# Weight rows in pairs, add and ReLU in one instruction, and another order in the first attention step

## The chip, the cores and the metric

The kernel runs on one core of a Trainium2 chip. Its metric is the device time of one execution in microseconds (us). The engines' names are those of the profile: PE does matrix multiplications (PEld is its loading of weights, instruction LDWEIGHTS), DVE is the vector engine, ACT the scalar engine, POOL the GpSimd engine, SP the sync engine. Matrix products land in PSUM, everything else lies in SBUF. POOL and SP issue DMAs here; POOL's convert fp32 in memory to fp16 in SBUF on the way.

## What is computed

A causal attention over 4 batches, 8 heads, 768 positions and 64 numbers per head, whose output feeds four experts that are all applied and mixed:

```python
is_retrieval = [1, 0, 1, 0, 0, 0, 1, 0]; n_sink, window = 4, 64
scores = q @ k.T / 8                  # per batch and head, 768 x 768
keep = causal                         # retrieval heads 0, 2, 6
keep = causal & (pos < 4 | rel < 64)  # the other, streaming heads
a = softmax(where(keep, scores, -1e9)); x = a @ v
x = x.transpose(0, 2, 1, 3).reshape(3072, 512)
p = domain_probs / (domain_probs.sum(-1) + 1e-9)
out = sum over e of p[:, e] * (relu(x @ w1[e]) @ w2[e])   # w1: 512 x 1024, w2: 1024 x 512
```

The output is fp32; products are taken in fp16 with fp32 accumulation.

## The kernel before

**Attention** is done in eight steps g = 2b + c, one for each batch b and each half c of its 768 positions (384 queries). `scores(h)` multiplies a head's keys and queries tile by tile into PSUM (L659), and ACT takes the exponential into an fp16 tile `es` (L677). For retrieval heads and c = 1 there are four such tiles, in the order of `score_tiles`: the first two cross the diagonal and are multiplied by a 0/1 mask on DVE (L681), the last two need no mask. In the first step (g = 0) the mask is added by a matmul instead (L671). `values(h)` multiplies the exponentials by v: for retrieval heads (`values_r`, L713) the result has a column with the sum, and DVE adds 1e-9, inverts and scales it (L738, L741, L742); for streaming heads (L785) the sums lie in PSUM beside the result, and ACT takes the logarithm (L803) and exp(-log) (L813; L818 for heads 3 and 4 of the first step together), after which DVE scales into `xT` (L808). That scaling is put off: `later` appends it to the list `behind`, and `tick` emits it on DVE when a planned 1.3 us have passed. `xT[g]` holds the step's output with the 512 columns in four tiles of 128 rows: tile 0 has heads 0 and 4, tile 1 heads 1 and 5, tile 2 heads 2 and 6, tile 3 heads 3 and 7. Retrieval heads' results have to be transposed to get there: in the first step by three matmuls with an identity and a copy on DVE (`x_transposes`, L762, L766). `both` interleaves two generators, step by step. PSUM tiles of the first step's values alternate between two buffers of `pV` and two of `pO`. The order of the first step's last part is written out by hand:

```python
yield from both(scores(6), values(4))
yield from both(scores(7), values(6))
yield from values(5)
yield from values(7)
x_transposes(6)
```

**The experts** work on 24 tiles of 128 rows of x. The first step's three tiles, and then the fourth alone, go through `plain_steps`, expert after expert: layer 1 (L1027: weights w1sb loaded, xT streamed with 384 or 128 columns) with the ReLU on ACT (L1040), layer 2 (L1048) with w2sb streamed, and the mix on DVE (L1060, L1064). The first four matmul groups of expert 0 take the column tiles in the order 0, 2, 1 for all four groups, and only then tile 3.

The other twenty tiles go in ten pairs through `pair_steps`. Layer 1 is a plain product (`plain_layer1`, L1154, 256 columns, ReLU on ACT L1163) for experts 0, 1, 2 in seven pairs and for experts 0, 1 in the last three; the rest, expert 3 or experts 2 and 3, are done with the seven products of Winograd's form (`winograd_layer1`, L1183), whose partial sums ACT keeps (L1193) and DVE adds (`add`: L1199) and cuts at zero (L1205). Layer 2 is the seven products over all experts at once (L1290). Between the pairs the attention steps 1 to 7 are fed in, piece by piece, by a plan.

**Loads of the weights** are all on POOL's queue, in an order written by hand, with `landed` (L502), a tiny copy on POOL that waits for an earlier load: w1 of expert 0, w2 of expert 0, w1 of 1, then `landed(w1_of(0))`, halves of the second step's k and q, `landed(w2_of(0))`, w2 of 1, and so on. `load_w1` makes two DMAs per expert with 2 KB rows in SBUF; `load_w2` (L339 to L343) one DMA with rows of 1 KB: SBUF partition p gets rows p, 128 + p, 256 + p, ... of w2[e], and the columns of w1 that are loaded for one LDWEIGHTS are accordingly 128 neighbours.

Of the kernel before, what the change touches and what calls it, by code (L numbers as in the profile page):

```python
# [9 lines left out]

# [8 lines left out]
def kernel(  # L19
# [311 lines left out]
    def load_w1(e, f0, f1):  # L331
        x = moe_w1[e].rearrange("(u c d) f -> u d c f", u=2, c=DMP)
        for u in range(2):
# [2 lines left out]
                in_=x[u, :, :, f0:f1],  # L336
            )

    def load_w2(e):  # L339
        gp.dma_start(  # L340
            out=w2sb[:, e * FTP : (e + 1) * FTP, :],
            in_=moe_w2[e].rearrange("(fo fi) d -> fi fo d", fi=P),
        )  # L343


    ONES = 0.0078125 * (1.0 + 15360.0 * 2.0**-23)
# [192 lines left out]
    def attention(b, c):  # L539
# [152 lines left out]
        def values_r(h):  # L692

            ct, u = PLACE[h]
            shared = by_dma and ct
            if not (shared and u):
                pv_of[0] = pV.tile([P, 512], FP32, name="pV", bufs=2)
            ps = pv_of[0]
            if first:
                warm_up(ps, {6: 6}.get(h, 0), 256)  # L700
            heads = ps.rearrange("p (u x) -> p u x", u=2)[:, :, 0 : 3 * (D + 2)]
            heads = heads.rearrange("p u (j x) -> p u j x", j=3)
            ps = heads[:, u if shared else 0, :, :]
            work = []
            for es, parts in es_of[h]:
                for t, o, q0, nq in parts:
                    for j in range(3):
                        x = j * P - q0
                        if 0 <= x < nq:
                            work.append((j, t, es[:, o + x : o + x + P]))  # L710
            ns = 0
            for n, (j, t, lhsT) in enumerate(work):
                nc.tensor.matmul(  # L713
                    out=ps[:, j, 0 : D + 1],
                    lhsT=lhsT,
                    rhs=vR[i][:, t, RH.index(h), 0 : D + 1],
                    start=(n == 0),
                    stop=(n == len(work) - 1),
                    skip_group_check=True,
                )  # L720
                ns += mm_ns(D + 1)
                if ns > 200 and n < len(work) - 1:
                    yield ns
                    ns = 0
            x = x_pair if ct else x_one
            if shared and not u:
                yield ns
                return
            if shared:
                rs = att.tile([P, 2, 3, 1], FP32, name="rs", bufs=2)  # L730
                sums, top = heads[:, :, :, D : D + 1], heads[:, :, :, 0:D]
                to = x.rearrange("p j (u d) -> p u j d", u=2)
                shape = [P, 2, 3, D]
            else:
                rs = att.tile([P, 2, 3, 1], FP32, name="rs", bufs=2)[:, 0, :, :]
                sums, top, to = ps[:, :, D : D + 1], ps[:, :, 0:D], x[:, :, half(u)]
                shape = [P, 3, D]
            nc.vector.tensor_scalar(  # L738
                out=rs, in0=sums, scalar1=1e-9, scalar2=None, op0=ALU.add
            )  # L740
            nc.vector.reciprocal(out=rs, in_=rs)  # L741
            nc.vector.tensor_tensor(  # L742
                out=to, in0=top, in1=rs.to_broadcast(shape), op=ALU.mult
            )
            yield ns
            if h != 2 and not first:
                nc.sync.dma_start(
                    out=xT[g][:, ct, :].rearrange("p (j x) -> p j x", j=3),
                    in_=x.rearrange("p j x -> p (j x)"),
                    transpose=True,  # L750
                )
# [85 lines left out]
        if first:  # L837
# [14 lines left out]
            yield from transposes(3)  # L852
            yield from values(1)
            yield from both(scores(5), values(3))
            yield from both(scores(6), values(4))
            yield from both(scores(7), values(6))
            yield from values(5)
            yield from values(7)
            x_transposes(6)
            tick(LAG)  # L860
            small_things()
        else:
# [83 lines left out]
    def tick(ns):  # L946
        clock[0] += ns
        while behind and behind[0][0] <= clock[0]:
            behind.pop(0)[1]()
# [64 lines left out]
    def plain_steps(nt0, tiles, e, tokens, n0):  # L1014
# [6 lines left out]
        for f0 in [0, *range(ahead, FTP)]:  # L1021
            pss = {ft: bank() for ft in range(f0, f0 + (1 if f0 else ahead))}
            cts = (0, 2, 1, 3)

            def layer1(ft, n):
                ct = cts[n]
                nc.tensor.matmul(  # L1027
                    out=pss[ft][:, 0:cols_n],
                    lhsT=w1sb[:, e * DMP + ct, ft * P : (ft + 1) * P],
                    rhs=x[:, ct, :],  # L1030
                    start=(n == 0),
                    stop=(n == DMP - 1),
                )

            for ft in pss:
                for n in range(DMP - 1):
                    layer1(ft, n)
            for ft, ps in pss.items():
                layer1(ft, DMP - 1)
                nc.scalar.activation(  # L1040
                    out=hs[:, ft, :], in_=ps[:, 0:cols_n], func=AF.Relu
                )
                yield DMP * mm_ns(cols_n), 0.6
# [88 lines left out]
    def first_sum(e, n=1):  # L1132
# [2 lines left out]
            out=S1[:, k, :], in0=A21[:, k, :], in1=A22[:, k, :], op=ALU.add  # L1135
        )


    PSHARE = 1.57

# [5 lines left out]
    def pair_steps(nt0, nxt):  # L1146

        def plain_layer1(e):
            xs = scaled(e)
            for f0 in range(0, FTP, 2):  # L1150
                ps = bank()
                for f in range(2):
                    for ct in range(DMP):
                        nc.tensor.matmul(  # L1154
                            out=ps[:, f * PC : (f + 1) * PC],
                            lhsT=w1sb[:, e * DMP + ct, (f0 + f) * P : (f0 + f + 1) * P],
                            rhs=xs[:, ct, :],
                            start=(ct == 0),
                            stop=(ct == DMP - 1),
                        )  # L1160
                b0 = 2 * (f0 // HT)
                k0 = e * HT + f0 % HT
                nc.scalar.activation(  # L1163
                    out=blocks[:, b0 : b0 + 2, k0 : k0 + 2, :].rearrange(
                        "p t f x -> p f t x"
                    ),
                    in_=ps.rearrange("p (f t x) -> p f t x", f=2, t=2),
                    func=AF.Relu,
                )
                yield 2 * DMP * mm_ns(PC), 0.5  # L1170
# [5 lines left out]
        def winograd_layer1(e, x, y):  # L1176
# [18 lines left out]
            def block(n):  # L1195
                return blocks[:, n, e * HT : (e + 1) * HT, :]

            def add(n, ps, b):
                nc.vector.tensor_tensor(  # L1199
                    out=block(b),  # L1200
                    in0=ps.rearrange("p (f x) -> p f x", f=HT),
                    in1=kept[n].rearrange("p (f x) -> p f x", f=HT),
                    op=ALU.add,
                )
                nc.vector.tensor_scalar(  # L1205
                    out=block(b), in0=block(b), scalar1=0.0, scalar2=None, op0=ALU.max
                )

            def t(n):
# [337 lines left out]
```

The softmax here doesn't subtract the row's maximum and nothing guards it: scores larger than these inputs give would overflow.

## Time and profile before

| | |
|---|---|
| three runs | 378.41, 378.68, 377.46 us, median 378.41 |
| profiled execution | 377.47 us; its span on the core 375.8 us |
| matmuls | 4128 |
| granted clock of PE | full over the whole span |
| w2 loads (L340) | 4, 11.7 to 16.5 us from issue to landing, median 12.5 |
| w1 loads (L334) | 8, 5.7 to 12.8 us, median 9.3 |
| mean DMA rate, 20 to 40 us | 201 GB/s |
| mean DMA rate, 60 us to the end | 89 GB/s |

The span is the time between the first and the last instruction on the core. Of PE it has to be known that matmuls are pipelined: a matmul's recorded time is that from its start to its end, while the next one has already started, so that "busy" hides short gaps. A timeline row merges neighbours of one kind ("x8"), and a bracket at its end says how long the engine had been idle before and what ended that.

### The profile page before, as it was taken

Reading aid. Unit: us, or ns where it says so; the run is one execution under the profiler, and the core shown is the slowest. Engines: PE = TensorE matmul, PEld = TensorE weight load, DVE = VectorE, ACT = ScalarE, POOL = GpSimd, SP = SyncE. Lnnn points to the kernel's source line nnn. Section 1 sums busy time; section 2 is a strip of 40 time slices with the busy share of each in tenths; the row PEclk is TensorE's granted clock in tenths of the full one; section 3 lists DMA queues with packets and bytes.
Section 4 is the critical chain, followed back from the end, with each engine's and each line's share of the span. In section 5 each row is a group of like instructions: output and inputs, shape, how many; then the busy total and the mean of one; then the engine's idle time right before and its main releaser. Section 6 shows DMA issues by size and latency. Waiting matters only on the chain.

```text
span 375.8 us, 10137 instructions
## 1 busy us (share of the span) xinstructions
PE 367.5 (98%) x4128; PEld 310.2 (83%) x4128; DVE 282.7 (75%) x620; ACT 227.8 (61%) x475; POOL 113.7 (30%) x155
## 2 busy tenths in 40 slices
PE   8889999999999999999999999999999999999996
PEld 4745466668998988999989898998899998999996
DVE  7774768697888679878758858967778868769572
ACT  3863478547785785765676955784777361450630
POOL 8934573882058038115601650320000000000000
PEclk9999999999999999999999999999999999999999
DMA  9999999999699599977904991951220300300101
GB/s 164 155 201 206 196 187 191 181 207 105 97 109 144 106 96 120 152 116 58 207 10 59 170 157 21 127 127 14 69 72 2 107 9 0 114 2 6 54 2 56
DMA packets 124771, 39.24 MB, mean 104 GB/s; under 512 B 113728, under 2 KB 118404, under 8 KB 124724
## 3 DMA queue, kind: packets, MB, share of 16 engines
q0 software_dynamic: 86848, 19.01, 59.1%
q1 hardware_dynamic: 36276, 19.18, 21.9%
q8 instruction: 32, 0.52, 0.6%
q10 hardware_dynamic: 1600, 0.39, 0.5%
q14 instruction: 15, 0.12, 0.1%
HBM read 44.89 MB, written 6.34 MB: 136 GB/s over the span
## 4 chain that ended last, share of the span: by engine, by line
PE 87%; DMA 7%; POOL 3%; DVE 2%; issue 0%; POOLq 0%
PE pO L1290 31%; PE pA L1154 25%; PE pO L1183 9%; DMA w2sb<-in_moe_w_dram 7%; PE pO L1048 6%; PE pA L659 5%; PE pA L1027 5%; PE pV L713 2%; PE pV L785 2%; PE pA L1183 2%; POOL vS L309 1%; POOL vR L303 1%; DVE xs L1112 1%; PE pA L1380 0%; POOL early L453 0%
## 5 line engine op out<-in xcount | busy, mean ns | idle before, releaser
L1290 PEld LDWEIGHTS <-hA 128*128 128x128 f16 x1104 | 104.9, 98 | 12.2
L1154 PE MATMUL pA<-xs,w1sb 128*128 128x256 f16 x864 | 109.3, 272 | 0.0
L1154 PEld LDWEIGHTS <-w1sb 128*128 128x128 f16 x864 | 80.7, 98 | 8.5
L1163 ACT ACTIVATE hA<-pA 128x512 f16<-128x512 f32 x108 | 64.4, 598 | 35.1 <-PE pA L1154 32.9
L1290 PE MATMUL pO<-w2sb,hA 128*128 128x256 f16 x640 | 76.7, 272 | 0.0
L677 ACT ACTIVATE es<-pA 128x384 f16<-128x384 f32 (+2 forms) x122 | 59.2, 511 | 27.1 <-PE pA L659 23.3
L305 POOL DMA_DIRECT2D vS<-in_v_dram x30 | 29.6, 989 | 111.7 <-PE pV L785 110.5
L1290 PE MATMUL pO<-tsb,hA 128*128 128x256 f16 x464 | 56.7, 272 | 0.0
L1112 DVE TENSOR_TENSOR xs<-xT,pB 128x1024 f16<-128x1024 f16 (+1 forms) x52 | 49.4, 969 | 1.2 <-DMA out_dram<-o 1.2
L967 DVE TENSOR_TENSOR hA<-hA 128x1024 f16<-128x1024 f16 x60 | 39.6, 684 | 0.4
L1040 ACT ACTIVATE hA<-pA 128x384 f16<-128x384 f32 (+1 forms) x64 | 22.2, 385 | 19.8 <-PE pA L1027 19.6
L1027 PE MATMUL pA<-xT,w1sb 128*128 128x384 f16 (+1 forms) x256 | 30.9, 273 | 1.3 <-DVE xT L766 0.8
L1048 PE MATMUL pO<-w2sb,hA 128*128 128x512 f16 x128 | 30.7, 379 | 0.3 <-DMA w2sb<-in_moe_w_dram 0.3
L1310 ACT COPY s<-pO 128x256 f32<-128x256 f32 x31 | 11.5, 372 | 27.7 <-PE pO L1290 21.9
L1027 PEld LDWEIGHTS <-w1sb 128*128 128x128 f16 x256 | 19.3, 98 | 10.2 <-issue 1.9
L808 DVE TENSOR_TENSOR xT<-pV,rc 64x384 f16<-64x384 f32 x37 | 20.5, 555 | 9.1 <-ACT rc L813 6.6
L1183 PEld LDWEIGHTS <-w1sb 128*128 128x128 f16 x416 | 26.3, 98 | 1.1 <-issue 0.2
L803 ACT ACTIVATE rc<-pV,eps 64x384 f32<-64x384 f32 x37 | 21.3, 576 | 6.5 <-PE pV L785 5.9
L1199 DVE TENSOR_TENSOR hA<-pO,s 128x512 f16<-128x512 f32 x26 | 17.9, 687 | 9.3 <-PE pO L1183 6.7
L681 DVE TENSOR_TENSOR es<-es,mS 128x384 f16<-128x384 f16 (+1 forms) x40 | 13.7, 343 | 13.4 <-ACT es L677 13.4
L659 PE MATMUL pA<-qT,kR 128*128 128x384 f16 (+2 forms) x120 | 22.9, 278 | 0.6 <-DVE kR L576 0.6
L1193 ACT COPY s<-pO 128x512 f32<-128x512 f32 x39 | 22.5, 585 | 1.4 <-PE pO L1183 1.2
(144 smaller groups left out, 498.2 us busy)
## 6 DMA issues: line engine op xcount, KB each, us to landing
pB<-p_rows SPq DMA_DIRECT2D x10, 512.0 KB
out_dram<-o SPq DMA_DIRECT2D x19, 256.0 KB
w1sb<-in_moe_w_dram POOLq DMA_DIRECT2D x8, 512.0 KB, 9.3
w2sb<-in_moe_w_dram POOLq DMA_DIRECT2D x4, 1024.0 KB, 12.5
vS<-in_v_dram POOLq DMA_DIRECT2D x30, 112.0 KB, 4.2
k_rows<-in_k_dram POOLq DMA_DIRECT2D x18, 128.0 KB, 5.6
q<-in_q_dram POOLq DMA_DIRECT2D x18, 128.0 KB, 6.4
vR<-in_v_dram POOLq DMA_DIRECT2D x24, 48.0 KB, 5.8
```

The costliest lines, as they stand in the source:

```text
L305: gp.dma_start(out=t[:, :, own_v(h)], in_=windows_of(v, b, h, c))
L659: nc.tensor.matmul(out=ps[:, o : o + nq], lhsT=key_tile(b, c, h, t), rhs=qTs[b, c][:, hp, q0 : q0 + nq], start=(n == 0 or not first), stop ...
L677: nc.scalar.activation(out=es[:, 0:cols], in_=ps[:, 0:cols], func=AF.Exp, scale=SC)
L967: nc.vector.tensor_tensor(out=out, in0=a, in1=b, op=ALU.subtract)
L1027: nc.tensor.matmul(out=pss[ft][:, 0:cols_n], lhsT=w1sb[:, e * DMP + ct, ft * P : (ft + 1) * P], rhs=x[:, ct, :], start=(n == 0), stop=(n = ...
L1048: nc.tensor.matmul(out=ps_o, lhsT=hs[:, ft, j * P : (j + 1) * P], rhs=w2sb[:, e * FTP + ft, :], start=(ft == 0), stop=(ft == FTP - 1),)
L1112: nc.vector.tensor_tensor(out=o, in0=xin, in1=pb.to_broadcast([P, DMP, n, P]), op=ALU.mult)
L1154: nc.tensor.matmul(out=ps[:, f * PC : (f + 1) * PC], lhsT=w1sb[:, e * DMP + ct, (f0 + f) * P : (f0 + f + 1) * P], rhs=xs[:, ct, :], start= ...
L1163: nc.scalar.activation(out=blocks[:, b0 : b0 + 2, k0 : k0 + 2, :].rearrange("p t f x -> p f t x"), in_=ps.rearrange("p (f t x) -> p f t x" ...
L1183: nc.tensor.matmul(out=ps[:, f * P : (f + 1) * P], lhsT=w[:, ct, f * P : (f + 1) * P], rhs=a[:, ct, :], start=(first and f == 0 and ct == ...
L1193: nc.scalar.copy(out=kept[n], in_=ps)
L1290: nc.tensor.matmul(out=ps, lhsT=a[:, k, :], rhs=b(k), start=(first and k == 0), stop=(k == KT - 1), skip_group_check=not first,)
```

## The change

It has five places.

- `load_w2`, for experts 0 and 1 (`in_pairs`): partition p gets rows 2p and 2p + 1 of each 256, so a row of the DMA has 2 KB in SBUF and 4 KB in memory. The order of the 1024 inner features is thereby another, and `w1_tile` takes w1's columns in the same order: every second one of 256, so that LDWEIGHTS reads fp16 elements with a step of two. It replaces the index at L1029 and L1156.
- `values_r`: for c = 1 the matmuls go through score tiles 2 and 3 first, then 0 and 1.
- The order of the first step: head 6's scores are done together, then head 7's with head 4's values, then head 6's values.
- At the end of the first step head 5's put-off scaling is taken from the list, and emitted after head 6's transposes and copy, which follow head 7's values.
- `add` in `winograd_layer1`: one custom DVE instruction computes max(min(a + b, 3.4e38), 0) in place of an add and a maximum.

```diff
     def load_w2(e):
-        gp.dma_start(
-            out=w2sb[:, e * FTP : (e + 1) * FTP, :],
-            in_=moe_w2[e].rearrange("(fo fi) d -> fi fo d", fi=P),
-        )
+        x = w2sb[:, e * FTP : (e + 1) * FTP, :]
+        if in_pairs(e):
+            gp.dma_start(
+                out=x.rearrange("p (m j) d -> p m (j d)", j=2),
+                in_=moe_w2[e].rearrange("(m p j) d -> p m (j d)", p=P, j=2),
+            )
+            return
+        gp.dma_start(out=x, in_=moe_w2[e].rearrange("(fo fi) d -> fi fo d", fi=P))
...
+    def in_pairs(e):
+        return e < 2
+
+    def w1_tile(e, ct, ft):
+        x = w1sb[:, e * DMP + ct, :]
+        if in_pairs(e):
+            x = x[:, ft // 2 * 2 * P : (ft // 2 + 1) * 2 * P]
+            return x.rearrange("p (x j) -> p j x", j=2)[:, ft % 2, :]
+        return x[:, ft * P : (ft + 1) * P]
...
-            for es, parts in es_of[h]:
+            tiles = es_of[h] if c == 0 else es_of[h][2:] + es_of[h][:2]
+            for es, parts in tiles:
...
-            yield from both(scores(6), values(4))
-            yield from both(scores(7), values(6))
+            yield from scores(6)
+            yield from both(scores(7), values(4))
+            yield from values(6)
             yield from values(5)
-            yield from values(7)
+            at_once = behind.pop()
+            v_steps = values(7)
+            yield next(v_steps)
             x_transposes(6)
+            at_once[1]()
+            yield from v_steps
             tick(LAG)
...
-                    lhsT=w1sb[:, e * DMP + ct, ft * P : (ft + 1) * P],
+                    lhsT=w1_tile(e, ct, ft),
...
-                            lhsT=w1sb[:, e * DMP + ct, (f0 + f) * P : (f0 + f + 1) * P],
+                            lhsT=w1_tile(e, ct, f0 + f),
...
-                nc.vector.tensor_tensor(
+                nc.vector._custom_dve(
+                    TENSOR_ADD_SAT,
                     out=block(b),
                     in0=ps.rearrange("p (f x) -> p f x", f=HT),
                     in1=kept[n].rearrange("p (f x) -> p f x", f=HT),
-                    op=ALU.add,
-                )
-                nc.vector.tensor_scalar(
-                    out=block(b), in0=block(b), scalar1=0.0, scalar2=None, op0=ALU.max
+                    s0=LARGEST,
+                    s1=0.0,
                 )
```

On each engine the number and order of the instructions is otherwise as before: on DVE 39 instructions fewer and head 6's copy ahead of head 5's scaling; on ACT head 6's second exponential and head 7's first ahead of head 4's logarithm; on PE head 6's second score tile and head 7's first ahead of head 4's values, and head 7's second ahead of head 6's values.

More of the change, by code (lines that the diff above doesn't have):

```diff
@@ L7 @@
 from concourse.act_sets import SETS
+from concourse.dve_ops import TENSOR_ADD_SAT
 from concourse._compat import with_exitstack
@@ L1136, in first_sum @@
         )
+    LARGEST = 3.4028234663852886e38
     PSHARE = 1.57
```

## The prediction

> **What bounds the kernel now.** I read the page first: the busy shares, then the chain that ended last.
>
> ```profile
> PE 367.5 (98%) x4128; PEld 310.2 (83%) x4128; DVE 282.7 (75%) x620; ACT 227.8 (61%) x475; POOL 113.7 (30%) x155
> PE 87%; DMA 7%; POOL 3%; DVE 2%; issue 0%; POOLq 0%
> ```
>
> PE is named almost throughout, but its busy time is modelled, so I laid the start times of the 4128 matmuls against what their columns take when dense: in the chain of waits, 16 matmuls of 128 columns take 0.89 us (55.6 ns each), 8 of 256 columns 0.87 (109 ns), 4 of 384 columns 0.65 (162 ns), 4 of 512 columns 0.86 (216 ns). What is left between the starts is 10.9 us: 7.2 us before 20 us, 1.9 from 20 to 40, 0.8 from 40 to 60, and only 1.0 in the 316 us after. So a change can win in the first 60 us and almost nowhere else, and it loses wherever it makes PE's stream itself slower. The waits of PE name the places:
>
> ```profile
> PE pV L713 <- ACT es L677: 1.0, 1, 1.0
> PE pA L1027 <- DVE xT L766: 0.8, 1, 0.8
> PE pV L713 <- DVE es L681: 0.6, 1, 0.6
> PE pO L1048 <- DMA w2sb<-in_moe_w_dram: 0.3, 1, 0.3
> ```
>
> The timeline of ACT, DVE and PE around the first two (start, us, engine, line, operation):
>
> ```profile
> 15.62 0.87 ACT L677 ACTIVATE es<-pA 128x256 f16<-128x256 f32 x2
> 16.52 0.57 ACT L803 ACTIVATE rc<-pO,eps 64x384 f32<-64x384 f32 x1
> 17.12 0.52 ACT L818 ACTIVATE rc<-rc 128x384 f32<-128x384 f32 x1
> 17.55 0.69 ACT L677 ACTIVATE es<-pA 128x256 f16<-128x256 f32 x2
> ...
> 18.26 0.56 DVE L808 TENSOR_TENSOR xT<-pO,rc 64x384 f16<-64x384 f32 x1
> 20.31 0.56 DVE L808 TENSOR_TENSOR xT<-pO,rc 64x384 f16<-64x384 f32 x1 [0.69 <-ACT rc L813]
> 20.90 0.56 DVE L766 CAST xT<-pV 128x384 f16<-128x384 f32 x1
> ...
> 17.97 0.24 PE L713 MATMUL pV<-vR,es 128*128 128x65 f16 x2 [1.03 <-ACT es L677]
> 20.37 0.32 PE L1027 MATMUL pA<-xT,w1sb 128*128 128x384 f16 x1 [0.36 <-DMA w1sb<-in_moe_w_dram]
> 21.52 2.60 PE L1027 MATMUL pA<-xT,w1sb 128*128 128x384 f16 x15 [0.82 <-DVE xT L766]
> ```
>
> The logarithm and reciprocal of heads 3 and 4 (L803, L818) stand on ACT ahead of head 6's second score tile; and head 6's copy into xT (L766) stands on DVE behind head 5's scaling.
>
> **Part 1, the order in the first step.** No instruction is added and none of those moved issues a DMA, so SP and POOL are passed by nothing. ACT now does head 6's second tile and head 7's first before L803 and L818 of head 4. Of the pair at 15.62 the second is a 512-wide exponential, 0.60, so it starts at 15.89; two such follow each other by 0.49 (1.09 for two at 41.35), a 256-wide one by 0.25 (0.69 less 0.44). Head 6's second tile starts at 16.38, head 7's first at 16.63, L803 at about 17.05, L818 0.60 later, at 17.65 instead of 17.12. PE's 1.03 us wait goes: head 6's values need a tile that is done at 16.77. But what waits for L818 is 0.55 late: heads 3 and 4's scalings on DVE (the second ends at 19.37, not 18.82), and behind them in DVE's order head 6's three normalising operations (end 20.17, not 19.62). Head 7's values take the PSUM buffer of head 4, so they too wait for 19.37; in the trace from there to head 6's transposes is 0.73 (18.95 to 19.68), so PE is there at 20.1 and waits for 20.2. Head 6's copy no longer stands behind head 5's scaling: 0.34 of transposes, then 20.57 to 21.13 (before: to 21.46); head 5's scaling follows, 21.16 to 21.72 (before: to 20.87), head 7's to 22.3. Layer 1 takes column tiles 0, 2, 1 and only after twelve matmuls 3. Before, one matmul is done and 31 are left at 21.52; after, tile 2 runs at 21.17, tile 1 at 21.77, with 30 left: 0.25 late less one matmul of 0.16. **+0.1 us**. The bounds: -1.0 if the wait removed reached layer 1 whole, +0.55 if all the delay did.
>
> **Part 2, two rows of w2 per partition for experts 0 and 1.** The same bytes in 512 packets of 2 KB instead of 1024 of 1 KB. In the trace's packet records, w2's 1 KB packets take 99 ns and w1's 2 KB packets 183 (median 173): per load 1024 x 99 = 101 engine-us against 512 x 183 = 94 (89), over 16 engines 6.3 against 5.9 (5.5) us, 0.5 to 0.7 less. The second load is issued when the first has landed, so it lands 1.0 to 1.5 earlier than 38.77. PE's wait there is 0.28; it would be at L1048 at 38.53, and with part 1 at 38.63, instead of 38.81: **-0.2 us for parts 1 and 2 together**. Without any gain of the DMA it stays at 38.81: 0.0. So the load covers what part 1 loses, or part 1's loss eats what the load gains.
>
> The Trainium skill, "DMA: Bandwidth & Descriptors", section Specifications, speaks against this part: transfers of 512 B and more are at line rate already. By it 1 KB packets cost no more per byte, the load lands at 38.77, and parts 1 and 2 come to nothing; the packet records above disagree a little (99 ns for 1 KB is more than half of 183), and I keep them.
>
> **The price of part 2: strided weights.** w1's columns must follow the same order, so LDWEIGHTS reads every second fp16 element for experts 0 and 1: 640 loads of L1154 (3 experts in seven pairs, of which two strided; both in the last three: 7 x 64 + 3 x 64), 64 beside matmuls of 384 columns and 64 beside 128 columns at L1027. No load in the trace is strided. From below: contiguous loads beside 65-column matmuls keep a period of 30 ns (L713, 7 in 0.21 us), so a strided load at half that speed is 60, and hidden under 109 and 162. From above: the loads that step 4 bytes per column, as these do:
>
> ```profile
> L557 PEld LDWEIGHTS pA<-early,hA 128*128 128x128 f32 x24 | 2.6, 144 | 1.3 <-POOL early L449 0.8 <-ACT es L677 0.3
> L1154 PEld LDWEIGHTS <-w1sb 128*128 128x128 f16 x864 | 80.7, 98 | 8.5
> ```
>
> L557's follow each other by 109 ns in the trace. At 109 the 640 are just hidden and the 64 beside 128 columns cost 64 x (109 - 55.6) = 3.4 us. I take 0, since the fp16 row with its 30 ns is the nearer one, and keep +3.4.
>
> The skill's "TensorE: Matmul & The Clock Gate", section Weight-path perf modes, allows the fast load for 128 non-fp32 columns at any column step up to 1,024 elements; by it the price is 0. By its section LDWEIGHTS, for a plain load (columns / 1.2, 107 ns), it would be about 3.3 us. No run here shows which holds.
>
> **Part 3, the order of the score tiles** in the value matmuls of heads 0, 2 and 6 of each second chunk, unmasked ones first:
>
> ```profile
> 42.23 0.76 PE L659 MATMUL pA<-qT,kR 128*128 128x128 f16 x5
> 42.65 1.47 ACT L677 ACTIVATE es<-pA 128x512 f16<-128x512 f32 x3 [0.21 <-PE pA L659]
> 43.22 0.42 DVE L681 TENSOR_TENSOR es<-es,mC 128x256 f16<-128x256 f16 x2
> 43.56 0.40 PE L713 MATMUL pV<-vR,es 128*128 128x65 f16 x7 [0.57 <-DVE es L681]
> ```
>
> Seven matmuls wait for DVE's masks. In the new order they need head 0's tiles 2 and 3 instead, which ACT makes at 42.65 to 43.25 and 43.14 to 43.63. So the stall moves from DVE to ACT: four matmuls at 43.27, three from 43.65, ending at 43.75, not 43.80: **-0.05 us**; at most -0.57. Other second chunks: PE waits for no score tile after 60 us.
>
> **Part 4, add and ReLU in one DVE instruction.**
>
> ```profile
> L1199 DVE TENSOR_TENSOR hA<-pO,s 128x512 f16<-128x512 f32 x26 | 17.9, 687 | 9.3 <-PE pO L1183 6.7 <-ACT s L1193 2.4
> L1205 DVE TENSOR_SCALAR hA<-hA 128x512 f16<-128x512 f16 x39 | 11.6, 298 | 1.3
> ```
>
> 39 instructions of 298 ns go, 11.6 us of DVE. The new one is not in the trace: 687 as the add alone, or 746 as L1064, the same size with a third operand; at most 39 x 59 = 2.3 us come back. PE's gaps after 60 us that are long enough to see are 0.07, 0.20, 0.26 and 0.16 (at 93, 140, 209 and 296 us); ahead of the last three DVE runs scalings, masks and input products, no L1205. So **0**; at most -0.6. What hides it is DVE's 25% of idle time: if the new one took twice the add, 39 x (1374 - 985) = 15 us more would fill a sixth of it.
>
> **Sum.** 0.1 and the load's gain make -0.2, the tiles -0.05, the rest 0: about -0.2 us. The profiled execution took 377.47 (span 375.8), so 377.2; the median of the three runs shown is 378.41, 0.94 above the profiled one, and with the same step it becomes **378.2 us**. The three runs lie 1.2 us apart; 0.3% (1.1 us) is about what can be told from no change.
>
> **Rivals.** *The front gives everything*: layer 1 a microsecond earlier, the load 1.0 to 1.5 earlier so that nothing holds it, masks off the path (-0.57), the late gaps gone (-0.6): -1.2 to -2.4, 376.0 to 377.2. For it: all the named waits are touched. Against: ACT's order above only moves the wait. *Strided weights show*: slower, at the 64 loads beside 128 columns, from a period of 55.6 ns on, and from 109 on at 640 more; at 109, +3.4 less 0.2: 381.6; at 73 ns it already costs 1.1. For it: PE has no slack to hide it. Against: loads at 30 ns leave a factor of 1.9. *The reordering loses*: scalings of heads 3 to 5 all late, +0.55, and the load no earlier; 378.7, within what can't be told; it takes a further stall to pass 1.1.
>
> **How the numbers follow.** The forecast, 0.51 (its own range 377.3 to 379.3); front gives everything 0.21; strided weights 0.23; reordering loses 0.05. Faster by over 0.3%: nearly all of the first rival, 0.21. Slower: strided weights and a little of the last and of the forecast's tail, 0.28. Within: 0.51. The range reaches to the bounds: 376.2 (most of -2.4) and 381.8 (+3.4).
>
> **What would show it.** Right: L1027's dense run at about 21.6 to 21.8 with a wait on DVE L808's line; no wait on w2sb at L1048; the first values of the second step waiting for ACT's es; LDWEIGHTS of w1sb at periods of 55.6 and 109 as before; DVE busy about 10 us less, PE's gaps after 60 us as they were. Wrong: periods over 56 ns in the 128-column matmuls of experts 0 and 1; the fused instruction well over 0.75 us; layer 1 dense before 21.0.

## The result and the profile after

| | time, us (median, lowest to highest, executions) |
|---|---|
| before | 378.36 (377.46 to 378.68, 4) |
| after | 378.07 (378.03 to 378.11, 4) |
| ratio after to before | 0.9996, 95% interval 0.9979 to 1.0014 |

No difference that can be told: forecast were 378.2 us and no change. The profiled execution of after took 378.03 us (before 377.47), its span is 376.3 us (before 375.8).

The busy shares and the chain that ended last, of after:

```profile
PE 368.2 (98%) x4128; PEld 310.5 (83%) x4128; DVE 271.6 (72%) x581; ACT 227.9 (61%) x475; POOL 111.9 (30%) x155
PE 94%; DVE 3%; ACT 2%; issue 0%; ACTq 0%
```

DVE has 39 instructions and 11.1 us less, PE is as full as before. The DMAs (7%) and POOL (3%) have left the chain, which says only where the backward walk happened to go in this execution. PE's waits of after:

```profile
PE pO L446 <- DVE xT L827: 1.4, 1, 1.4
PE pO L446 <- DVE early L431: 1.3, 1, 1.3
PE pA L676 <- DVE kR L593: 0.6, 2, 0.4
PE pV L732 <- ACT es L694: 0.3, 1, 0.3
PE pA L1051 <- DVE xT L785: 0.3, 1, 0.3
PE pA L1051 <- DVE xT L827: 0.3, 1, 0.3
```

The 1.0 us wait of head 6's values for ACT is gone, and 1.4 us stand a little later: PE waits for DVE's scalings of heads 3 and 4 (L827), which free the buffer for head 7. The 0.8 of layer 1 has become 0.3 and 0.3, the 0.6 for the masks 0.3 for ACT, and there is no wait on w2sb. The timeline of after around the end of the first step:

```profile
15.82 1.48 ACT L694 ACTIVATE es<-pA 128x256 f16<-128x256 f32 x4
17.32 0.57 ACT L822 ACTIVATE rc<-pO,eps 64x384 f32<-64x384 f32 x1
17.93 0.52 ACT L837 ACTIVATE rc<-rc 128x384 f32<-128x384 f32 x1
...
18.48 0.55 DVE L827 TENSOR_TENSOR xT<-pV,rc 64x384 f16<-64x384 f32 x1 [2.43 <-ACT rc L837]
19.06 0.56 DVE L827 TENSOR_TENSOR xT<-pO,rc 64x384 f16<-64x384 f32 x1
20.85 0.56 DVE L785 CAST xT<-pV 128x384 f16<-128x384 f32 x1 [0.43 <-PE pV L781]
...
19.68 0.50 PE L446 MATMUL pO<-early 128*128 128x256 f16 x3 [1.38 <-DVE xT L827]
20.86 0.32 PE L1051 MATMUL pA<-xT,w1sb 128*128 128x384 f16 x1
21.46 0.32 PE L1051 MATMUL pA<-xT,w1sb 128*128 128x384 f16 x1 [0.28 <-DVE xT L785]
22.05 2.11 PE L1051 MATMUL pA<-xT,w1sb 128*128 128x384 f16 x12 [0.27 <-DVE xT L827]
```

This execution was late already ahead of the part that changed: the first score matmul starts at 6.61 us, at 6.36 before, and ACT's exponentials of the row at 15.82, the last that both orders have in the same place, stand at 15.62 before. Take these last 0.20 us off, and ACT's logarithm stands at 17.12 and L837 at 17.73, the second scaling ends at 19.42, layer 1's second matmul starts at 21.26 and the dense run at 21.85.

The second attention step of after, where the order of the score tiles has changed:

```profile
42.17 0.76 PE L676 MATMUL pA<-qT,kR 128*128 128x128 f16 x5
42.59 1.47 ACT L694 ACTIVATE es<-pA 128x512 f16<-128x512 f32 x3 [0.21 <-PE pA L676]
43.16 0.42 DVE L698 TENSOR_TENSOR es<-es,mC 128x256 f16<-128x256 f16 x2
43.24 0.65 PE L732 MATMUL pV<-vR,es 128*128 128x65 f16 x7 [0.31 <-ACT es L694]
```

The seven matmuls start 0.31 us late in place of 0.57, but spread over 0.65 us in place of 0.40: the last three stand still for the next tile. Counted from layer 2 of expert 1 (38.81 us before, 38.75 after), all seven are done 0.01 us sooner, no more.

And by shape, the fused instruction and the strided weight loads of after:

```profile
L1226 DVE CUSTOM_DVE_ANT_0 hA<-pO,s 128x512 f16<-128x512 f32 x26 | 17.7, 689 | 12.5 <-PE pO L1209 8.8 <-ACT s L1219 3.3
L1180 PEld LDWEIGHTS <-w1sb 128*128 128x128 f16 x864 | 80.7, 98 | 8.5
```

689 ns against 687 for the add alone, and 98 ns for a weight load as before.

The two traces can be laid beside each other at four places. Matmuls are called dense here where each starts as soon as the columns of the one before allow. Layer 1's dense run, taken back to its first matmul at 162.5 ns each, starts at 21.35 us before and 21.73 after; layer 2 of expert 1 at 38.81 and 38.75; the last matmul at 372.65 and 372.72; from there to the end of the span it is 3.11 and 3.59 us. So in this pair of executions the change lost 0.38 us in front, got it back at the load of w2, lost 0.13 between there and the last matmul, and 0.48 in the tail. The experiments show which of these four belong to the change.

### The profile page after: what moved, and what is told of

Read it like the earlier page. It is cut to its first block, busy times and chain, and to the rows that moved or that the text cites. A ratio compares the mean times of both kernels' runs of the same rounds, so it can differ in the third digit from the quotient of the medians.

```text
span 376.3 us, 10100 instructions
## 1 busy us (share of the span) xinstructions
PE 368.2 (98%) x4128; PEld 310.5 (83%) x4128; DVE 271.6 (72%) x581; ACT 227.9 (61%) x475; POOL 111.9 (30%) x155
## 4 chain that ended last, share of the span: by engine, by line
PE 94%; DVE 3%; ACT 2%; issue 0%; ACTq 0%
PE pO L1316 31%; PE pA L1180 25%; PE pO L1209 9%; PE pA L1051 7%; PE pO L1072 7%; PE pA L676 5%; PE pV L732 2%; PE pV L804 2%; PE pA L1209 2%; PE pO L446 1%; ACT es L694 1%; PE pA L574 1%; DVE xT L827 1%; DVE xs L1136 1%; PE pA L1406 0%; ACT rc L822 0%
## 5 line engine op out<-in xcount | busy, mean ns | idle before, releaser
L1136 DVE TENSOR_TENSOR xs<-xT,pB 128x1024 f16<-128x1024 f16 (+1 forms) x52 | 49.5, 970 | 1.8 <-DMA xT<-x_pair 1.7
L1336 ACT COPY s<-pO 128x256 f32<-128x256 f32 x31 | 11.5, 372 | 27.7 <-PE pO L1316 21.9
L827 DVE TENSOR_TENSOR xT<-pV,rc 64x384 f16<-64x384 f32 x37 | 20.5, 555 | 10.5 <-ACT rc L832 7.5
L1226 DVE CUSTOM_DVE_ANT_0 hA<-pO,s 128x512 f16<-128x512 f32 x26 | 17.7, 689 | 12.5 <-PE pO L1209 8.8
```

The costliest lines, as they stand in the source:

```text
L827: nc.vector.tensor_tensor(out=xT[g][r, ct, :], in0=ps[r, 0:CH], in1=rc[r, :], op=ALU.mult)
L1136: nc.vector.tensor_tensor(out=o, in0=xin, in1=pb.to_broadcast([P, DMP, n, P]), op=ALU.mult)
```

## The experiments

Each ran beside further runs of the kernel before on the same chip: 377.46 us (median of 35) for the four single parts; 377.48 (28) for the first kernel with blocks, four rows, the order taken apart and head 6 first; 377.49 (29) for the other four.

**One part alone.** Each of the four parts was put into the kernel before by itself.

*The order of the first step.*

```diff
-            yield from both(scores(6), values(4))
+            yield from scores(6)
+            yield from both(scores(7), values(4))
...
+            at_once = behind.pop()
...
```

> Part 1 alone (the new order of the first step), all else as before. My theory (the parts hardly matter one by one, because PE's stream is full and ACT only hands the wait on): layer 1 of expert 0 is dense 0.1 to 0.4 us later than before, PE then reaches expert 1's layer 2 when its weights have just landed (about 38.8 us), so the time is that of before within 0.4 us. Rival (the parts cancel: the order gains what another part loses): layer 1 dense 0.5 to 1 us earlier, and the time 0.3 to 1 us less.

Measured: 377.63 us, ratio 1.0001 (0.9985 to 1.0017).

*Two rows per partition, with strided weights.*

```diff
-            in_=moe_w2[e].rearrange("(fo fi) d -> fi fo d", fi=P),
+                in_=moe_w2[e].rearrange("(m p j) d -> p m (j d)", p=P, j=2),
...
```

> Part 2 alone (two rows of w2 per partition for experts 0 and 1, strided weights). My theory: periods of the matmuls with strided weights stay 55.6 and 109 ns, expert 1's w2 lands 0.5 to 1 us earlier, the wait of 0.28 us before layer 2 of expert 1 is gone: 0.2 to 0.4 us less time. Rival (the strided loads cost and something else pays for them): 128-column periods of expert 0 and 1 of 60 to 109 ns, time 0.3 to 3.4 us more.

Measured: 377.23 us, ratio 0.9986 (0.9964 to 1.0008).

*Add and ReLU fused.*

```diff
-                nc.vector.tensor_tensor(
+                nc.vector._custom_dve(
+                    TENSOR_ADD_SAT,
...
```

> Part 4 alone (add and ReLU in one instruction). My theory: one fused instruction takes 0.69 us like the add, DVE's busy time falls by 11 to 12 us, PE's gaps after 60 us stay at 1.0 us in sum, and the time is that of before within 0.3 us. Rival (the vector engine sets part of the time): the gaps at 140, 209 and 296 us shrink, 0.3 to 0.6 us less.

Measured: 377.30 us, ratio 0.9993 (0.9978 to 1.0008).

*The order of the score tiles.*

```diff
-            for es, parts in es_of[h]:
+            tiles = es_of[h] if c == 0 else es_of[h][2:] + es_of[h][:2]
```

> Part 3 alone (unmasked score tiles first). My theory: the first values of the second step wait for ACT in place of DVE and are done 0.05 us earlier; the gap of 0.13 us at 118 us that the changed kernel has appears here too; the time is that of before within 0.3 us. Rival (the masks were in the way): 0.5 us less.

Measured: 377.54 us, ratio 0.9997 (0.9981 to 1.0013).

No part alone can be told from no change, and the times alone decide nothing. The traces do, at the four places named above (us):

| kernel | first score matmul | layer 1 dense | layer 2 of expert 1 | from there to the last matmul | from there to the end |
|---|---|---|---|---|---|
| before | 6.36 | 21.35 | 38.81 | 333.84 | 3.11 |
| after | 6.61 | 21.73 | 38.75 | 333.97 | 3.59 |
| order alone | 6.79 | 21.92 | 38.93 | 333.85 | 3.10 |
| rows alone | 6.20 | 21.34 | 38.36 | 333.85 | 3.10 |
| fused alone | 6.79 | 21.74 | 38.75 | 333.85 | 3.10 |
| tiles alone | 6.79 | 21.74 | 38.75 | 333.98 | 3.11 |

Three kernels happen to start their scores at 6.79: with the new order layer 1 is dense at 21.92, without it at 21.74 twice. So part 1 costs 0.18 us. Counted from ACT's exponentials just ahead of the changed part (15.62 us in before) it is the same in more executions: 5.73 or 5.74 us to the dense run in all six with the old order, 5.91 or 5.92 in the three with the new one (after, order alone, and four rows further down). The column before the last is the same to 0.01 us in all executions of this table without the new tile order, and 0.13 more in those with it, so strided weights and the fused instruction cost and bring nothing there, and the tile order costs 0.13. Where, the value matmuls at 118 us show, in the timeline of before first, then of after:

```profile
117.97 0.38 PE L659 MATMUL pA<-qT,kR 128*128 128x128 f16 x2
118.19 0.38 PE L713 MATMUL pV<-vR,es 128*128 128x65 f16 x7
118.40 0.39 PE L659 MATMUL pA<-qT,kR 128*128 128x256 f16 x2
```

```profile
117.89 0.38 PE L676 MATMUL pA<-qT,kR 128*128 128x128 f16 x2
118.11 0.52 PE L732 MATMUL pV<-vR,es 128*128 128x65 f16 x7
118.46 0.38 PE L676 MATMUL pA<-qT,kR 128*128 128x256 f16 x2
```

Seven matmuls take 0.52 us in place of 0.38. ACT makes the unmasked tiles last, and here the masks were done at 117.77 before, ahead of the first of these matmuls: the new order asks for the latest tile first, and the last three matmuls wait until ACT has made it at 118.30. At 42 us the same order moved a stall from DVE to ACT and gained 0.01.

**What a stride of the weights costs.** Blocks of 48 matmuls of 64 columns, which at about 29 ns each are too short to hide a load that needs the 55.6 ns of a 128-column matmul, were put into the changed kernel after the first step, with weights read at steps of 1, 2 and 4 elements.

```diff
+    for step in (1, 2, 4):
+        for n in range(48):
+            nc.tensor.matmul(
+                out=ps_m[:, 0:64],
+                lhsT=warm.rearrange("p (x j) -> p j x", j=step)[:, 0, 0:P],
+                rhs=warm[:, 0:64], start=True, stop=True,
+            )
```

> The disputed price by itself: the changed kernel with 144 more matmuls of 64 columns after the first step, 48 each with weights that step 1, 2 and 4 fp16 elements; they compute nothing that is used. My theory (a step costs a load nothing): the same period of about 29 ns for all three, so 4.2 us are added at most. Rival (a step of two halves the load's rate and was hidden under 56 and 109 ns): about 30 ns for step 1, 45 to 60 for step 2, 100 or more for step 4.

Measured: 384.07 us (one execution). The first block could not be read: it ran at a granted clock of 0.50, as the table of three windows over the blocks shows (window: its length, PE busy and count, PEld busy and count, granted clock, DMA share, GB/s):

```profile
21.50:23.40 1.90, 1.76 (x34) 1.76 (x34) 0.50 1.12 215
23.40:25.40 2.00, 2.00 (x56) 2.00 (x54) 0.73 1.11 183
25.40:27.40 2.00, 2.00 (x65) 1.96 (x61) 1.00 1.09 197
```

So step 1 took 52.7 ns per matmul here, step 2 a median of 29 and step 4 of 33, where 29 had been expected for all three. It was done again with more blocks:

```diff
-    for step in (1, 2, 4):
+    for step in (1, 1, 1, 2, 4, 1, 2, 4):
```

> The changed kernel with 8 blocks of 48 matmuls of 64 columns each after the first attention step, whose weights are read with steps 1, 1, 1, 2, 4, 1, 2, 4; the first two or three blocks are there to bring the clock back. Theory A (a step of two is free): at full clock, blocks with steps 1 and 2 both at 29 to 30 ns per matmul; step 4 at 33 ns. Rival B (a step of two is slower and only hidden): 31 ns or more for step 2 against 29 for step 1. Time about 390 us (378 and 384 matmuls, of which some 70 at half clock).

Measured: 394.21 us (one execution). From start to start, at full clock: the four blocks of step 1 29.1 to 29.2 ns, both of step 2 a median of 29 and no single one over 30 (but for one pause), step 4 33 ns twice. A weight load of step 2 is as fast as a plain one, with nothing hidden; step 4 is 14% slower. The time lies above the expected 390 because PE stood still twice inside the blocks, for 1.6 and 2.3 us (last section).

**Four rows per partition in place of two**, so that weights have step 4 in the kernel itself, experts 0 and 1 (`load_w2` gets `j=4` likewise):

```diff
-            x = x[:, ft // 2 * 2 * P : (ft // 2 + 1) * 2 * P]
-            return x.rearrange("p (x j) -> p j x", j=2)[:, ft % 2, :]
+            x = x[:, ft // 4 * 4 * P : (ft // 4 + 1) * 4 * P]
+            return x.rearrange("p (x j) -> p j x", j=4)[:, ft % 4, :]
```

> The changed kernel with four rows of w2 per partition in place of two, for experts 0 and 1: packets of 4 KB, weights that step four elements. My theory: a 4 KB packet takes 340 to 350 ns against twice 173 to 183, so expert 1's w2 lands at most 0.3 us earlier, which PE does not wait for any more, and the stepping costs nothing: the same time within 0.3 us. Rival (a step costs something that 55.6 and 109 ns hid): periods over 56 ns at 128 columns and over 109 at 256, 1 us more and up to 10.

Measured: 379.06 us, ratio 1.0031 (1.0017 to 1.0046): the only version that is slower than before beyond its interval, where the same time had been expected. But not at the weights: matmuls beside them keep their periods of 55.8, 109.2 and 162.5 ns, though the load of expert weights now takes 109 ns on average:

```profile
L1180 PEld LDWEIGHTS <-w1sb 128*128 128x128 f16 x864 | 87.7, 109 | 2.6
```

The profiled execution has one new gap of PE, 0.75 us at 248 us, where DVE's input products (L1136) start 1.5 us later than in after (0.3 of it by the shift of the whole run), behind a DMA. That the eleven times fall into two groups, 378.0 to 378.5 and 379.1 to 379.7, fits a gap that is there in some executions only; why it comes was not settled. A gap of 0.61 us at 253 us stands in the first kernel with the blocks, whose expert weights have step 2, so step 4 is not needed for one.

**The order of the first step taken apart.** In the changed kernel, head 4's and head 6's work was put back into the old order, and only the copy into xT kept ahead of head 5's scaling:

```diff
-            yield from scores(6)
-            yield from both(scores(7), values(4))
-            yield from values(6)
+            yield from both(scores(6), values(4))
+            yield from both(scores(7), values(6))
```

> The changed kernel without the reordering of head 6's scores and head 4's values; head 6's copy still comes ahead of head 5's scaling. My theory (head 6's scores together push the logarithm of head 4 back and lose what the copy's new place wins): layer 1 of expert 0 dense 0.4 to 0.7 us earlier than in the changed kernel, measured from the first score matmul; the time 0 to 0.5 us less, since expert 1's w2 lands no earlier. Rival (the reordering of head 6 is what helps): layer 1 dense later than in the changed kernel, and the time 0.2 to 0.6 us more.

Measured: 377.83 us, ratio 1.0002 (0.9990 to 1.0014). The old wait is back, 1.06 us of head 6's values for ACT, and layer 1 is dense at 21.37 us though this execution started its scores at 6.96: 0.37 before the two executions with the old copy order that started 0.17 earlier. From ACT's exponentials ahead of the changed part to the dense run it takes 5.30 us, against 5.73 with the old copy order and 5.91 with the whole of part 1. So the copy by itself brings 0.43 us in front, and the order of the scores loses 0.61, together the 0.18 of part 1. Here the first layer-1 matmul, at 20.82, waited 0.38 us for w1 of expert 0: that load was the next thing in the way. The copy's order alone, without the new tiles, was not run.

**Head 6 first of all.** The put-off scalings were held back until head 6's values were normalised, and its transposes went ahead of head 7's values:

```diff
+            hold.append(1)
             yield from both(scores(7), values(4))
             yield from values(6)
-            yield from values(5)
-            at_once = behind.pop()
-            v_steps = values(7)
-            yield next(v_steps)
+            hold.clear()
+            tick(LAG)
+            x_steps = values(5)
+            yield next(x_steps)
             x_transposes(6)
-            at_once[1]()
-            yield from v_steps
+            yield from x_steps
+            yield from values(7)
...
-        while behind and behind[0][0] <= clock[0]:
+        while behind and not hold and behind[0][0] <= clock[0]:
```

> The changed kernel with the scalings of heads 3 and 4 held back until head 6 is normalised, and head 6's transposes ahead of head 7's values. My theory (the reordering lost because head 6's normalising stood behind those scalings on the vector engine): layer 1 dense about 1 us earlier than in the changed kernel; but PE then waits for w2 of expert 0 or 1, which land at about 26 and 38.2 us whatever the front does, so the time is only 0.2 to 0.6 us less. Rival (the front alone sets the time): 1.0 us less and no wait on a load.

Measured: 377.81 us, ratio 1.0004 (0.9992 to 1.0016), so the gain that was expected can't be seen in the times. Layer 1 is dense at 20.62 us, 1.1 earlier than after, and yet the last matmul starts at 372.67, where after's is at 372.72. PE's waits of this kernel:

```profile
PE pV L577 <- DMA q<-in_q_dram: 0.5, 1, 0.5
PE pO L1074 <- DMA w2sb<-in_moe_w_dram: 0.4, 1, 0.4
...
PE pA L1053 <- DMA w1sb<-in_moe_w_dram: 0.2, 1, 0.2
```

None of these three loads held PE in after. The wait for w1 comes ahead of the dense run; those for q and w2 take the 1.1 us back (by start times, laid against rows alone, 0.55 and 0.52), and layer 2 of expert 1 starts at 38.70 against 38.75.

**The same without the load of w2 of expert 1.** If the loads bind, taking one of them away should let the microsecond through. The load is left out, expert 0's w2 stands in for it in every product, and what waited for it on POOL's queue waits for a load of q instead.

```diff
-    load_w2(1)
...
-    landed(w2_of(1))
+    landed(qt16[0:1, HP, 0, 0:1])
...
-                    rhs=w2sb[:, e * FTP + ft, :],
+                    rhs=w2sb[:, w2_at(e) * FTP + ft, :],
```

> The version that starts layer 1 a microsecond earlier (head 6 first), but w2 of expert 1 is left out: its load is not issued, and expert 0's w2 stands in its place in every product. Theory A (the loads bind the front, so an earlier layer 1 is given back at w2 and q): layer 2 of expert 1 starts 17.0 us after layer 1's dense run, at about 37.6 in place of 38.7, the last matmul at about 371.6 in place of 372.7; time about 1 us less than with the load, 376.8 us, ratio about 0.998. Rival B (something else at the end of the first 40 us takes the microsecond, the scores of the second step for example): last matmul at 372.4 or later, time as before, 377.4 to 377.8.

Measured: 377.68 us, ratio 1.0001 (0.9985 to 1.0018), and layer 2 of expert 1 at 38.70 again, not 37.6; the last matmul at 373.09. The expectation was missed. The timeline of PE in it:

```profile
21.09 5.61 PE L1055 MATMUL pA<-xT,w1sb 128*128 128x384 f16 x32 [0.47 <-DMA w1sb<-in_moe_w_dram]
33.71 0.36 PE L579 MATMUL pV<-ident,q 128*64 128x128 f16 x6 [0.47 <-DMA q<-in_q_dram]
38.70 1.03 PE L1076 MATMUL pO<-w2sb,hA 128*128 128x512 f16 x4
```

The wait at w2 is gone, as it must be, but this execution waits 0.47 us for w1 of expert 0 and 0.47 for q of the second step, both of which stand ahead of the left-out load in POOL's queue and could not profit from it. So it is shown that loads take the front's microsecond (both waits name one), but the w2 load is only the last of several; and a gap of 0.40 us at 79 us, where a matmul waits for DVE's work on w2sb, stands in this kernel alone.

**The kernel before, once more**, to see what a wait of 0.3 us in one profile is worth. No edit.

> The kernel before itself, unchanged, to see by how much its own executions differ. Theory A (the place at which a run's first score tile starts and the time at which w2 of expert 1 lands are scatter of the loads): about 377.5 us, ratio 0.999 to 1.001 with an interval about as wide as those of the single parts (0.0026 to 0.0044); in the profile the first score matmul starts anywhere from 6.2 to 7.0 us, w2 of expert 1 has its last packet anywhere from 37.9 to 38.5, and the 0.28 us wait of layer 2 for it need not be there. Rival B (rows of 1 KB make the load late): last packet at 38.5 again and a wait of about 0.3 us again.

Measured: 377.45 us, ratio 0.9996 (0.9980 to 1.0012). PE's waits in this profile of the unchanged kernel:

```profile
PE pO L429 <- DVE early L414: 1.3, 1, 1.3
PE pA L1027 <- DVE xT L766: 1.1, 1, 1.1
PE pV L713 <- ACT es L677: 1.0, 1, 1.0
PE pA L659 <- DVE kR L576: 0.8, 3, 0.4
PE pV L713 <- DVE es L681: 0.6, 1, 0.6
PE pA L557 <- DMA hA<-in_q_dram: 0.2, 1, 0.2
```

The wait on w2sb is not among them: its last packet comes at 38.00 us, not at 38.50, and the last matmul starts at 372.24 in place of 372.65. The first score matmul starts at 6.19 us (what moves it stands in the last section). The wait was one execution's, not the kernel's. Rows alone, with layer 2 of expert 1 at 38.36, had looked like the expected gain; here it starts at 38.38 without the new rows. Where the last packet of this load comes, in ten executions: without the new rows 38.50, 38.00, 37.98, 38.04 and 38.08, with them 37.93, 37.91, 38.11, 38.36 and 38.24: means of 38.12 and 38.11. From the load's issue to its last packet it takes 11.51 us without and 11.66 with them (medians of the same ten). The rows of 2 KB make the load no earlier. The rows of 4 KB have their last packet at 37.64 in their one profile, but there the load was issued early, and from issue to last packet it took 11.49.

**The two parts that cost nothing, without the other two**: the kernel before with the rows and the fused instruction.

> The kernel before with two rows per partition and the fused add and ReLU, without the new order of the first step and without the new order of the score tiles. Theory A (the tiles' order costs 0.13 us at 118 us and gains nothing at 42, the first step's order costs 0.2): 333.85 us from layer 2 of expert 1 to the last matmul (333.97 with the new tile order), and 0 to 0.4 us below the kernel with the whole change: 377.3 us, ratio 0.998 to 1.000. Rival B (the parts help each other): 0.3 us or more above the whole change, 378.1 or more.

Measured: 377.43 us, ratio 0.9996 (0.9980 to 1.0011). From layer 2 of expert 1 to the last matmul it takes 333.85 us, as expected. Against the whole change (0.9996 in its own comparison) nothing can be told from the times. No version of this study is faster than the kernel before beyond its interval.

**The tail.** All seven kernels that hold the rows, the fused instruction, the new tiles and head 6's copy ahead of head 5's scaling together (after and those made from it, but for the one with only the rows and the fused instruction) take 3.44 to 3.59 us from the last matmul's start to the end; the seven with fewer of them 3.10 or 3.11. The last two DVE instructions, before and then after:

```profile
372.09 0.29 DVE L1387 TENSOR_TENSOR o<-pA,s 128x128 f32<-128x128 f32 x1 [0.54 <-PE pA L1380]
372.91 0.29 DVE L1387 TENSOR_TENSOR o<-pA,s 128x128 f32<-128x128 f32 x1 [0.53 <-PE pA L1380]
```

```profile
372.50 0.29 DVE L1413 TENSOR_TENSOR o<-pA,s 128x128 f32<-128x128 f32 x1 [0.89 <-PE pA L1406]
372.98 0.29 DVE L1413 TENSOR_TENSOR o<-pA,s 128x128 f32<-128x128 f32 x1 [0.18 <-PE pA L1406]
```

The first add of the output's last rows runs 0.41 us later, and the last two output DMAs, on one queue, are issued 0.48 us apart in place of 0.79; issuing the last one takes 0.74 us in place of 0.33. The bracket names PE, but in the semaphore events of after PE's count came at 372.06 and ACT's, the other one it waits for, at 370.35. So it stood still for 0.4 us after both had come. Something else goes with it in all fourteen traces. DVE's records, those of its sequencer included, number 746 in before, rows alone and tiles alone, 745 with part 1 alone, 710 with the fused instruction without part 1 (two kernels) and 709 in the seven with the long tail. The last 8 KB packet on q14, a queue that the profile calls "instruction", moves with this number: about 23 us before the last matmul's start at 746 and 745, 2.1 us before it at 710, and 0.5 to 0.8 us behind it at 709. So the fused instruction and the copy's new place together, which set this number, fit the long tail; the rows and the tiles, which leave it as it is, do not. That the add stands still because DVE's next instructions are not there yet was not tried, and the cause stays open.

## Why the prediction was right, and where it was not

The verdict, no change that can be told, was right. That the time came so near (378.07 for 378.2) is in part luck. The forecast stood on 378.41, the median of three runs of the kernel before. Its 92 later runs, in three sets, have medians of 377.46 to 377.49, and only 15 of them lie above 378.3. By the traces the change did not win 0.2 us but lost some 0.8. Against these figures a start 0.9 too high and a step 1.0 too low made up for each other. Why the first runs lay so high stays open, and after was not run again beside the later ones. The rivals with gains or losses beyond 1 us did not come. Point by point:

*Part 1, +0.1 us at layer 1*: right, 0.18, and right within 0.1 us in each step once the 0.20 us of the later start are taken off: logarithm 17.12 for 17.05, L837 17.73 for 17.65, second scaling 19.42 for 19.37, tile 2 at 21.26 for 21.17, the dense run 21.85 for 21.77. What the prediction did not name is that w1 of expert 0 bounds the gain of any order here: in five of the six executions with the old one the first layer-1 matmul waited for this load, until 20.4 to 21.1 us, which is 0.5 to 1.2 us ahead of the dense run.

*Part 2, the load 1.0 to 1.5 us earlier, parts 1 and 2 together -0.2*: **this step failed**. The packets cost what was read off (98 and 173 to 183 ns), and yet the load lands when it did: means of 38.12 and 38.11. Counting the packets' own time over 16 engines gave 6.3 us for a load that takes 11.5 from its issue to its last packet; that it shares the engines with other loads fits (in before the recorded times of all packets from 20 to 40 us add up to 1.32 times that of the 16 engines), but was not tested by itself. The Trainium skill, "DMA: Bandwidth & Descriptors", section Specifications, has transfers from 512 B at line rate already. The prediction had set the packet rows above it, and the landing times agree with the rule. And the wait that the step was to remove was chance: the second profile of the unchanged kernel has none. It was also read too short: 0.28 us is the idle time behind the modelled end of the matmul before, by start times the wait cost 0.45 (17.46 us from the dense run to layer 2 of expert 1, 17.02 with rows alone).

*Strided weights, 0*: right. Periods of 55.8, 109.1 and 162.5 ns as before, and 29 ns even with nothing to hide behind. The Trainium skill's "TensorE: Matmul & The Clock Gate", section Weight-path perf modes, by which the fast load holds for steps up to 1,024 elements, agrees with the blocks at step 2. At step 4 they took 33 ns for 29, so such a load is not quite free. The upper bound of 109 ns, from fp32 loads that step 4 bytes, did not hold for fp16: step 2 is 4 bytes too, and took 29.

*Part 3, -0.05*: wrong in sign, +0.13. The stall at 42 us moved from DVE to ACT as worked out, but the seven matmuls then ended 0.01 sooner, not 0.05: the last of them had started at 43.77 before, not at the 43.80 that the prediction compared with. And the sentence that PE waits for no score tile after 60 us was true only of the old order: the new one made such a wait, at 118 us.

*Part 4, 0*: right. 689 ns for 687, DVE 11.1 us less, the late gaps at 140, 209 and 296 us unchanged (0.20, 0.26 and 0.16 us).

*The sum, -0.2*: not shown, and by the traces nearer to +0.8: 0.18 and 0.13, and 0.48 in the tail, a term that the prediction did not have. The times of whole executions are too coarse to show it (intervals of 0.0024 to 0.0044, so 0.9 to 1.7 us wide); the unchanged kernel against itself gave 0.9996. The profiled pair differs by 0.56 us (377.47 to 378.03), nearly all of it the tail's 0.48: what the change lost ahead of the tail was almost covered by the chance wait for w2 in the profile of before.

## What to carry to other kernels

A wait of a few tenths in one profile may belong to that execution: profile the unchanged kernel twice before a change is made for it, and compare intervals between fixed events rather than ends: from layer 2 of expert 1 to the last matmul they agreed here to 0.01 us. Begin such an interval at the last event ahead of the changed part. Where a stream of loads runs under the work, moving the compute up moves the wait to the next load; see first which load is the next to bind. An order chosen for the one step that waits for a mask (0.01 us gained) can cost another step whose masks are hidden (0.13 lost).

## What was not expected of the hardware

- The first score matmul of an execution started between 6.15 and 7.04 us in fourteen profiles of nearly the same front. It is not the loads: the six transposes of the first k and q ahead of it start at 4.65 to 4.88 us in all of them. But they follow each other after the first about 109 ns apart in the four executions with the earliest scores (6.15 to 6.36) and about 213 ns apart in the eight with the latest (6.77 to 7.04), and the trace's first record of a full granted clock starts at 4.0 to 4.9 us in the early ones, at 5.5 and 5.6 in the two between, and at 6.2 to 7.2 in the late ones (one has no such record). So it is PE's clock, coming up sooner or later, that moves this start, as far as the traces show.
- PE stood still twice within a run of 384 equal matmuls that wait for nothing (28.03 to 29.71 and 33.60 to 35.91 us from start to start). On q8, a queue of the kind "instruction" that has 32 packets of 16 KB in the kernels with 4128 matmuls and 35 here, packets begin at 27.46 and 33.49. That PE had no instructions fits; it was not tried. The waits of PE in the second kernel with the blocks:

```profile
PE pO L1469 <- issue: 3.6, 2, 2.1
```

- After a pause of 1.2 us PE's granted clock was 0.50 in one kernel (from 21.09 to 24.50 us; 52.7 ns for 64 columns) and full in the other, which had the same pause at the same place (1.2 us, then 29.1 ns).
- A custom DVE instruction with add, minimum and maximum takes what the add alone takes: 689 and 687 ns for 128 x 512 with an fp32 operand in PSUM.
